# Splitting the planes of a burst around the next half round's first sum, in the two-tile stage of an FFT convolution

## The chip, the cores and the metric

The kernel runs on one core of one Trainium2 chip. The metric is the device time of one execution in microseconds (us); less is better. One core has a matrix engine (PE, with its weight loads shown as PEld), a vector engine (DVE), a scalar engine (ACT), a general engine (POOL) and a queue engine (SP) that issues the DMAs here. Every engine works through its own instructions strictly in the order in which the program gives them; engines wait for each other by semaphores.

## The reference

```
def reference(x, w):                       # x (1, 224, 224, 96), w (7, 7, 96, 96), bfloat16
    wp = jnp.pad(w, ((0, H - K), (0, W - K), (0, 0), (0, 0)))
    Xf = rfft2(x, axes=(1, 2)); Wf = rfft2(wp, axes=(0, 1))      # float32
    Yf = jnp.einsum('bhwi,hwio->bhwo', Xf, Wf)
    y = irfft2(Yf, s=(H, W), axes=(1, 2)).astype(jnp.bfloat16)
```

So it is a circular 7 x 7 convolution with 96 channels in and out on a picture of 224 x 224, with padding that wraps around.

## The kernel before

The rows of the picture are cut into 8 bands of 28 (`NJ`, `B`), each taken with 6 rows of its neighbour, so that a band has 34 values along h (`L`). Along h a band is transformed by a small real transform with 17 frequencies (`NS`); along w the convolution is done directly, pair of pixels by pair, with a scheme that saves products: it needs sums and differences of neighbouring columns, the planes. The width is cut into seven tiles of 32 columns (t = 0 to 6). Per tile there are four kinds of work:

- The forward transform: matmuls from the pixels `xn` with the matrix `Fm` into PSUM, evacuated to `xf` (`a_jobs`, `f_jobs`).
- The planes: `jit(t, g)` (line 476) makes, for a group of three frequencies, seven planes `J` from `xf` by three DVE instructions: four differences in one instruction (96x1824 for three frequencies, 96x1216 for two), one sum (96x456), and two sums of planes (96x912). There are three buffers `J`, used in turn.
- The products: `b_round(t, s, mid, end, ydve, planes)` (line 529), one call for each tile and frequency s. This text calls a call a half round. Its PE part is 19 matmuls into a PSUM bank `b0` (line 557), then the jobs of `mid()`, then 14 matmuls into a bank `b1`, then the jobs of `end()`. ACT reads `b0` into `tt_` (line 604), DVE makes the first sum `u` from `b0` and `tt_` (line 607), DVE makes `v` from `b1` and `tt_` (line 617), and POOL makes the result `yf` from `u` and `v` (`ysum`, line 620). The tiles `u`, `v` and `tt_` have two buffers each (`tv_pool`, line 779): the u of a half round is written into the place that the sum of the half round two earlier reads, and tt_ into the place that the v of two half rounds earlier reads. The two frequencies s = 0 and s = 16 (`REAL`) take a shorter path without u and POOL: DVE adds straight into `yf`.
- The inverse transform: `yf` goes through DRAM (`scr`), comes back as `tt` and is multiplied by `Gm`; the result is stored.

PSUM has eight banks; all banks come from one pool (line 106), and each new use of a bank waits until the readers of its last use are done. Which physical bank a use gets is settled when the program is built.

The order of the work is written out by hand. Tiles 0 and 1 are worked on together (the loop at line 816): in round r tile 0 does frequency r and tile 1 frequency r - 4 (`LAG`), so that most rounds have two half rounds, tile 0's ahead of tile 1's. In this two-tile stage the remaining weights are prepared as well: matmuls from `wq` (`prep_jobs`, line 349), evacuations into `WF`, and at the end of each group two or three DVE instructions `diff` (line 380, 96x960, WF<-WF). These, and the forward transform of tiles 1 and 2, are the jobs that `mid()` and `end()` hand out. From tile 2 on the tiles run one after the other (the loop at line 864).

The planes of a group are made in one half round, its burst: `bursts` (line 807) holds twelve of them, keyed by round and tile; eleven of them fall to tile 0 and tile 1 and the last one is `jit(2, 0)` in round 18. Two of the twelve come in REAL half rounds: round 4, tile 1 (s = 0), and round 16, tile 0 (s = 16). In a burst the planes follow v on DVE (line 629), and POOL's sum of that half round is made to wait for the last of them (line 634). They are wanted three half rounds later or more.

Who evacuates a bank, DVE or ACT, is decided when the program is built: `evac` (line 119) gives it to the engine with the smaller running estimate in `load`; every job and every plane instruction adds to that estimate at the moment at which it is recorded. At line 639 the finished `yf` of three frequencies is stored to `scr`, behind the jobs of `end()`.

Of the kernel before, what the change touches and what calls it, by code (L numbers as in the profile page):

```python
# [10 lines left out]
ALU = mybir.AluOpType  # L11
# [7 lines left out]
REAL = (0, NS - 1)  # L19
# [36 lines left out]
def kernel(  # L56
# [7 lines left out]
    _, H, W, C = x.shape  # L64
    assert tuple(w.shape) == (KT, KT, C, C) and C == 96 and H == NJ * B and W % (2 * TW) == 0
    NT = W // (2 * TW)
    TL = NT - 1
# [7 lines left out]
    SYNC = mybir.DependencyInfo(mybir.DependencyClass.Sync, mybir.DependencyReason.DATA)  # L75
# [19 lines left out]
    VE, SE, GE, TE, DE = (_Ordered(e) for e in (nc.vector, nc.scalar, nc.gpsimd, nc.tensor, nc.sync))  # L95
# [37 lines left out]
    def dma(out_ap, in_ap):  # L133
        return DE.dma_start(out=out_ap, in_=in_ap)

    WF = cpool.tile([128, NSLOT, NTAP, C], BF16, name="WF")
    PP = POS * NJ
# [123 lines left out]
    for r, n, v in ((0, 0, 1.0), (0, LC, -1.0), (1, 1, -1.0), (1, L - 1, 1.0)):  # L261
        o = mf[:, :, 2 * NS - 2 + r:2 * NS - 1 + r]
# [213 lines left out]
    def jit(t, g):  # L476
        s0, s1 = JGB[g]
        n = s1 - s0
        xf = xf_tiles[t][0:C]
        xv = xf.rearrange("c p r s w j -> c p r s (w j)")  # L480
        b = jcount[0] % 3 if t < 2 else (jcount[0] - 2 * len(JGB)) % 2
        jcount[0] += 1
        Jb = J_bufs[b][0:C].rearrange("c (k s q) -> c k s q", k=7, s=3)
        for s in range(s0, s1):
            jbuf[(t, s)] = Jb[:, :, s - s0]

        def sub(o, a, b, op, cost):
            def f():
                load["v"] += 170 + cost / 1.92
                return VE.tensor_tensor(out=o, in0=a, in1=b, op=op)  # L490
            return f
        x0, x1 = xv[:, 0, :, s0:s1], xv[:, 1, :, s0:s1]
        c0, c1 = max(s0, REAL[0] + 1), min(s1, REAL[1])
        i0, i1 = c0 - s0, c1 - s0
        pd, rd, sd, qd = x1.ap
        dpl = bass.AP(x1.tensor, x1.offset - NJ, [pd, [NJ, 2], rd, sd, qd])
        return [
            sub(Jb[:, 0:4, 0:n].rearrange("c (k r) s q -> c k r s q", r=2), dpl,
                x0.unsqueeze(1).to_broadcast([C, 2, 2, n, PP]), ALU.subtract, 4 * PP * n),
            sub(Jb[:, 4, i0:i1], xv[:, 0, 0, c0:c1], xv[:, 0, 1, c0:c1], ALU.add, PP * (c1 - c0)),  # L500
            sub(Jb[:, 5:7, i0:i1], Jb[:, 0:4:2, i0:i1], Jb[:, 1:4:2, i0:i1], ALU.add, 2 * PP * (c1 - c0)),
        ]
# [16 lines left out]
        return ops  # L519

    yf_cur = {}

    def pairs(ap):
        return ap.rearrange("p (r g o) -> p g r o", r=2, o=2)

    def yp(ap):
        return ap.rearrange("p g (r o) -> p g r o", o=2)

    def b_round(t, s, mid, end, ydve=False, planes=()):
        xf = xf_tiles[t][0:C]  # L530
        Jb = jbuf[(t, s)]
# [9 lines left out]
        else:  # L541
# [3 lines left out]
            yf, y0, y1 = yf_cur[t]  # L545
# [14 lines left out]
        if s in REAL:  # L560
            for part in range(2):
                conv(b0, part * C, 0, part)
            if t == TL:
                SE.copy(out=tt_.rearrange("p (r m o) -> p r m o", r=2, m=2),
                        in_=b0[:, 0:2 * C].rearrange("p (r o) -> p r o", o=C).unsqueeze(2).to_broadcast([128, 2, 2, C]))
            else:
                SE.copy(out=tt_[:, 0:2 * C], in_=b0[:, 0:2 * C])
            mid()
            for mi, m in enumerate((2, 1)):
                for part in range(2):  # L570
                    conv(b1, (part * 2 + mi if t == TL else mi * 2 + part) * C, m, part)
            if t == TL:
                VE.tensor_tensor(out=yp(ym), in0=pairs(tt_[:]), in1=pairs(b1[:, 0:4 * C]), op=ALU.add)
            else:
                VE.tensor_tensor(out=ym,
                                 in0=tt_[:, 0:2 * C].rearrange("p (r o) -> p r o", o=C).unsqueeze(1).to_broadcast([128, 2, 2, C]),
                                 in1=b1[:, 0:4 * C].rearrange("p (m r o) -> p m r o", m=2, r=2), op=ALU.add)
            load["a"] += 110 + 0.9 * 192
            load["v"] += 540
            for f in planes:  # L580
                f()
            end()
        else:
            v = tv_pool.tile([128, 2, 2, C], F32, name="v")
            if merge:
                conv(b0, 2 * C, 0, 0, both=True)
                conv(b0, 2 * C, 2, 0, add=True)
                conv(b0, 3 * C, 1, 0, add=True)
                conv(b0, 0, 0, 1)
                conv(b0, C, 0, 2)  # L590
                SE.mul(out=tt_[:], in_=b0[:, 0:4 * C], mul=-0.5)
                u, pr = tt_[:, 2 * C:4 * C].rearrange("p (m o) -> p m o", m=2), tt_[:, 0:2 * C]
            else:
                for part in range(3):
                    conv(b0, part * C, 0, part)
                conv(b0, 3 * C, 2, 0)
                conv(b0, 4 * C, 1, 0)
                u = tv_pool.tile([128, 2, C], F32, name="u")
                if t == TL:
                    SE.mul(out=tt_[:, 0:C], in_=b0[:, 0:C], mul=-0.5)  # L600
                    SE.copy(out=tt_[:, C:3 * C], in_=b0[:, C:3 * C])
                    load["a"] += 240
                else:
                    SE.mul(out=tt_[:, 0:3 * C], in_=b0[:, 0:3 * C], mul=-0.5)
                pr = tt_[:, C:3 * C]
            if not merge:
                VE.scalar_tensor_tensor(out=u[:], in0=b0[:, 3 * C:5 * C].rearrange("p (m o) -> p m o", m=2), scalar=-0.5,
                                        in1=tt_[:, 0:C].unsqueeze(1).to_broadcast([128, 2, C]), op0=ALU.mult, op1=ALU.add)
            mid()
            for mi, m in enumerate((2, 1)):  # L610
                for pi, part in enumerate((1, 2)):
                    conv(b1, (pi * 2 + mi if t == TL else mi * 2 + pi) * C, m, part)
            if t == TL:
                VE.tensor_tensor(out=v[:], in0=pr.rearrange("p (r o) -> p r o", r=2).unsqueeze(2).to_broadcast([128, 2, 2, C]),
                                 in1=b1[:, 0:4 * C].rearrange("p (r m o) -> p r m o", r=2, m=2), op=ALU.add)
            else:
                VE.scalar_tensor_tensor(out=v.rearrange("p m r o -> p m (r o)"),
                                        in0=pr.unsqueeze(1).to_broadcast([128, 2, 2 * C]), scalar=-2.0,
                                        in1=b1[:, 0:4 * C].rearrange("p (m q) -> p m q", m=2), op0=ALU.mult, op1=ALU.add)
            def ysum(eng):  # L620
                if t == TL:
                    return eng.tensor_tensor(out=yp(ym), in0=pairs(v.rearrange("p r m o -> p (r m o)")),
                                             in1=u.rearrange("p m (g o) -> p (m g) o", o=2).unsqueeze(2).to_broadcast([128, C, 2, 2]), op=ALU.add)
                return eng.tensor_tensor(out=ym, in0=v[:],
                                         in1=u.unsqueeze(2).to_broadcast([128, 2, 2, C]), op=ALU.add)
            if ydve:
                ysum(VE)
            last = None
            for f in planes:
                last = f()  # L630
            if not ydve:
                y = ysum(GE)
                if last is not None:
                    tc.add_manual_dep(y.ins, last.ins.name, SYNC, reason="sum after planes")
            load["a"] += 490 if merge else 410
            load["v"] += (560 if ydve else 250 if t < 2 else 0) + (560 if merge else 900)
            end()
        if t != TL and s == y1 - 1:
            dma(scr_tiles[t].rearrange("w j s e -> (w j) s e")[:, y0:y1], yf[:, 0:y1 - y0].rearrange("p s r m o -> p s (r m o)"))

    scr_tiles = {}
# [29 lines left out]
    def turn_a(i):  # L671
        src = xn_all[:, 0:NA].bitcast(F32).rearrange("p (g k s) -> p g k s", k=2, s=SR)
        turn(src, xs[:, 0:NA], i * C // 8, (i + 1) * C // 8)
# [96 lines left out]
    last = [f() for f in fj[0][1]]  # L770
# [3 lines left out]
    for f in jit(0, 0):  # L774
        f()
# [40 lines left out]
    for r in range(NS + LAG):  # L816
# [31 lines left out]
        for t in range(2):  # L848
            s = r - LAG * t
            if not 0 <= s < NS:  # L850
                continue
            now = bursts.pop((r, t), ())
            now = jit(*now) if now else ()
# [10 lines left out]
    for t in range(2, NT):  # L864
# [19 lines left out]
        for s in range(NS):  # L884
            now = ()
            if s in plan:
                g = plan[s]
                now = jit(t, g + 1) if g + 1 < len(JGB) else jit(t + 1, 0)
# [5 lines left out]
            if t == TL and s in LROUND:  # L894
                now = late_planes(LROUND[s])
            if t == TL and s >= SA:
                if s < NS - 1:
                    now = [lambda i=s - SA: turn_a(i)]
# [30 lines left out]
    for i, (j, h) in enumerate(order):  # L929
# [3 lines left out]
        k = i + 8 - LF  # L933
# [38 lines left out]
```

## Time and profile before

| What | Before |
|---|---|
| Median of 3 runs | 264.38 us (264.13 to 265.65) |
| The profiled execution's own time | 264.4 us |
| Its span in the profile | 262.7 us |
| PE, busy share of the span | 96% |
| DVE | 81% |
| ACT | 76% |
| POOL | 40% |

The span is the time from the first to the last instruction that the profiler saw; 1.7 us of the execution's own time lie around it. A busy share is an average over the whole span. The page also has a chain of waits: from the last instruction back, at every step to what released it. Nearly all instructions carry line 88 in the profile, the line of the wrapper that records them, so they are told apart by what they write and read, as in `J<-xf`. All times of places in this text are us from the start of the span.

### The profile page before, as it was taken

The numbers are of one execution on the slowest core, as the hardware profiler recorded it, in microseconds if no ns is written. First come the engines' busy times: TensorE is split into PE (matmuls) and PEld (weight loads), VectorE is DVE, ScalarE is ACT, GpSimd is POOL, SyncE is SP. The second block draws the span as 40 slices with busy tenths as digits, with TensorE's granted clock in tenths as the row PEclk, the third lists the DMA queues.
The fourth block names the chain that finished last, engine by engine and source line by source line (L and its number), as shares of the span: only waits on it lengthen the run. The fifth ranks groups of instructions, "written<-read, shape, count | busy, mean of one in ns | idle before, by whom it ended". The sixth has DMA issues, their size and how long they took to land.

```text
span 262.7 us, 12200 instructions
## 1 busy us (share of the span) xinstructions
PE 251.7 (96%) x5156; PEld 233.9 (89%) x5156; DVE 214.0 (81%) x456; ACT 198.4 (76%) x500; POOL 106.3 (40%) x170
## 2 busy tenths in 40 slices
PE   8899898999999999999999999999999999999981
PEld 3679898999999999999999998999999999999861
DVE  5657899897979969977988788777978889889982
ACT  5558897659785666998988879989798886666662
POOL 7782042336355652234133322643143222555621
PEclk9999999999999999999999999999999999999998
DMA  6848010641111299997978549698959853495145
GB/s 167 250 124 218 11 49 2 170 146 50 47 47 47 95 267 191 259 246 201 299 222 216 162 128 302 195 265 204 297 190 209 228 160 134 131 175 167 52 116 175
DMA packets 41416, 43.44 MB, mean 165 GB/s; under 512 B 30836, under 2 KB 33104, under 8 KB 41362
## 3 DMA queue, kind: packets, MB, share of 16 engines
q1 hardware_dynamic: 41044, 41.98, 57.8%
q8 instruction: 40, 0.66, 1.1%
q0 software_dynamic: 192, 0.52, 0.7%
q10 hardware_dynamic: 126, 0.17, 0.2%
q14 instruction: 14, 0.11, 0.1%
HBM read 22.09 MB, written 19.66 MB: 159 GB/s over the span
## 4 chain that ended last, share of the span: by engine, by line
PE 76%; POOL 7%; DVE 7%; issue 5%; ACT 4%; DVEq 0%; POOLq 0%; ACTq 0%
PE pb L88 76%; POOL ct L88 6%; DVE WF L88 2%; ACT WF L88 2%; DVE J L88 1%; DVE u L88 1%; ACT xf L88 1%; DVE xf L88 1%; DVE v L88 1%; POOL yf L88 1%; DVE yf L88 0%; ACT tt L88 0%; ACT tt__1860 L88 0%; ACT ct L88 0%; ACT tt__2947 L88 0%
## 5 line engine op out<-in xcount | busy, mean ns | idle before, releaser
L88 PE MATMUL pb<-WF,J 96*128 96x96 bf16 x2782 | 160.4, 206 | 0.8 <-DVE WF L88 0.7
L88 PEld LDWEIGHTS <-J 96*128 96x128 bf16 x2782 | 136.1, 98 | 9.0 <-DVE u L88 1.5
L88 POOL TENSOR_TENSOR yf<-v,u 128x384 bf16<-128x384 f32 x70 | 69.7, 1009 | 128.0 <-issue 68.5
L88 ACT CAST xf<-pb 96x408 bf16<-96x408 f32 (+3 forms) x143 | 67.1, 488 | 9.0 <-PE pb L88 7.2
L88 PE MATMUL pb<-WF,xf 96*128 96x96 bf16 x991 | 61.7, 206 | 1.1 <-ACT xf L88 0.5
L88 DVE TENSOR_TENSOR J<-xf 96x1824 bf16<-96x1824 bf16 (+1 forms) x82 | 56.9, 732 | 0.1
L88 PEld LDWEIGHTS <-xf 96*128 96x128 bf16 x991 | 49.0, 98 | 2.0 <-issue 1.0
L88 PE MATMUL pb<-Fm,xn 118*128 118x136 bf16 (+3 forms) x640 | 45.5, 199 | 0.9 <-DVE u L88 0.8
L88 ACT CAST WF<-pb 96x480 bf16<-96x480 f32 (+1 forms) x59 | 29.1, 573 | 4.5 <-PE pb L88 4.5
L88 PE MATMUL pb<-tt,Gm 102*84 102x384 bf16 (+1 forms) x132 | 32.1, 326 | 0.0
L88 PEld LDWEIGHTS <-xn 118*128 118x128 bf16 x640 | 30.5, 97 | 1.2 <-issue 1.1
L88 ACT CAST yo<-pb 84x384 bf16<-84x384 f32 (+1 forms) x66 | 28.2, 484 | 2.9 <-PE pb L88 2.9
L88 ACT CAST J<-pb 84x384 bf16<-84x384 f32 (+1 forms) x65 | 28.0, 484 | 3.0 <-PE pb L88 3.0
L88 DVE TENSOR_TENSOR J<-J 96x912 bf16<-96x912 bf16 (+2 forms) x41 | 22.5, 548 | 0.0
L88 PE MATMUL pb<-wq 98*128 98x120 bf16 (+1 forms) x288 | 21.3, 226 | 0.2 <-issue 0.2
L88 PEld LDWEIGHTS <-wq 98*128 98x128 bf16 x288 | 19.3, 148 | 0.6 <-issue 0.6
L88 POOL TENSOR_TENSOR xn<-v,u 128x384 bf16<-128x384 f32 x12 | 10.9, 923 | 9.5 <-DVE J L88 6.5
L88 PEld LDWEIGHTS <-Gm 102*84 102x84 bf16 (+1 forms) x132 | 11.1, 117 | 1.0 <-DMA tt<-scr 0.2
L88 DVE TENSOR_TENSOR yf<-v,u 128x384 bf16<-128x384 f32 x20 | 11.3, 567 | 0.7
L88 PE MATMUL pb<-wu 128*128 128x512 bf16 x39 | 10.6, 432 | 1.1 <-DVE ct L88 1.1
L88 ACT COPY xf<-xf 96x816 bf16<-96x816 bf16 (+3 forms) x20 | 11.2, 622 | 0.0
L88 DVE CAST WF<-pb 96x480 bf16<-96x480 f32 (+1 forms) x13 | 7.5, 611 | 4.3 <-PE pb L88 4.1
(404 smaller groups left out, 253.9 us busy)
## 6 DMA issues: line engine op xcount, KB each, us to landing
scr<-yf SPq DMA_DIRECT2D x30, 288.0 KB
xn<-in_x_dram SPq DMA_DIRECT2D x12, 672.0 KB
tt<-scr SPq DMA_DIRECT2D x24, 336.0 KB
out_dram<-yo SPq DMA_DIRECT2D x12, 252.0 KB
out_dram<-J SPq DMA_DIRECT2D x12, 252.0 KB
tt<-scr SPq DMA_DIRECT2D x6, 288.0 KB
WF<-in_x_dram SPq DMA_DIRECT2D x2, 672.0 KB
scr<-yf SPq DMA_DIRECT2D x6, 192.0 KB
```

Of the source, the lines that this page charges most:

```text
L88: r = fn(*a, **k)
```

## The change

In tiles 0 and 1 the first plane instruction (four planes) is cut into two instructions of two planes. In a half round with u and with planes, in the two-tile stage, only the first instruction of the planes' list is recorded behind v; `end()` follows, and everything else of the burst (the other plane instructions, POOL's sum, and the store to `scr`, if the half round closes a group) is put into a list `rest`. The next half round records it right behind its u and ahead of its `mid()`. In the two REAL bursts all plane instructions stay together. For `jit(2, 0)` the first instruction is not cut; the two others move. In the later tiles the planes stay where they were, but the store to `scr` is recorded ahead of `end()` now.

```
@@ jit
+        cut = ((0, 2),) if t > 1 else ((0, 1), (1, 2))
         return [
-            sub(Jb[:, 0:4, 0:n].rearrange("c (k r) s q -> c k r s q", r=2), dpl,
-                x0.unsqueeze(1).to_broadcast([C, 2, 2, n, PP]), ALU.subtract, 4 * PP * n),
+            sub(Jb[:, 2 * a:2 * b, 0:n].rearrange("c (k r) s q -> c k r s q", r=2), dpl[:, a:b],
+                x0.unsqueeze(1).to_broadcast([C, b - a, 2, n, PP]), ALU.subtract, 2 * (b - a) * PP * n) for a, b in cut] + [
...
+    rest = []
+
+    def go_on():
+        while rest:
+            rest.pop(0)()
...
@@ b_round, both paths
+            go_on()
             mid()
...
@@ b_round, path with u
-            last = None
-            for f in planes:
-                last = f()
-            if not ydve:
-                y = ysum(GE)
-                if last is not None:
-                    tc.add_manual_dep(y.ins, last.ins.name, SYNC, reason="sum after planes")
+            now = min(len(planes), 1) if t < 2 else len(planes)
+
+            def finish():
+                last = None
+                for f in planes[now:] if now < len(planes) else ():
+                    last = f()
+                if not ydve:
+                    y = ysum(GE)
+                    last = last or done[0]
+                    if last is not None:
+                        tc.add_manual_dep(y.ins, last.ins.name, SYNC, reason="sum after planes")
+                if t != TL and s == y1 - 1:
+                    dma(scr_tiles[t].rearrange("w j s e -> (w j) s e")[:, y0:y1], yf[:, 0:y1 - y0].rearrange("p s r m o -> p s (r m o)"))
+            done = [None]
+            for f in planes[0:now]:
+                done[0] = f()
+            if now < len(planes):
+                rest.append(finish)
+            else:
+                finish()
...
             end()
-        if t != TL and s == y1 - 1:
+        if t != TL and s == y1 - 1 and s in REAL:
             dma(scr_tiles[t].rearrange("w j s e -> (w j) s e")[:, y0:y1], yf[:, 0:y1 - y0].rearrange("p s r m o -> p s (r m o)"))
```

On DVE a burst so goes from "v, planes, u of the next half round" to "v, half of the first, u of the next half round, the other half, the other two".

More of the change, by code (lines that the diff above doesn't have):

```diff
@@ L608, in b_round @@
                                         in1=tt_[:, 0:C].unsqueeze(1).to_broadcast([128, 2, C]), op0=ALU.mult, op1=ALU.add)
+            go_on()
             mid()
```

## The prediction

> **What bounds the kernel now.** I read the page first: the shares of the engines and the chain of waits.
>
> ```profile
> span 262.7 us, 12200 instructions
> ...
> PE 251.7 (96%) x5156; PEld 233.9 (89%) x5156; DVE 214.0 (81%) x456; ACT 198.4 (76%) x500; POOL 106.3 (40%) x170
> ...
> PE 76%; POOL 7%; DVE 7%; issue 5%; ACT 4%; DVEq 0%; POOLq 0%; ACTq 0%
> ```
>
> PE sets the time: whatever makes it stand still is added to the end, and a faster DVE is worth only the stalls that it takes away. The change works from 20 to 97 us, so I cut that into windows (us, then busy us and instruction counts for PE, PEld, DVE, ACT, POOL, then clock and DMA).
>
> ```profile
> 20.00:35.00 15.00, 13.97 (x328) 13.77 (x329) 12.69 (x24) 13.55 (x34) 3.45 (x5) 1.00 0.40 101
> 35.00:50.00 15.00, 14.01 (x348) 13.78 (x344) 14.18 (x28) 10.92 (x29) 4.02 (x4) 1.00 0.22 68
> 50.00:65.00 15.00, 14.91 (x338) 14.79 (x337) 13.29 (x26) 11.99 (x29) 6.92 (x8) 1.00 0.36 112
> 65.00:80.00 15.00, 14.95 (x343) 14.86 (x340) 12.58 (x24) 11.66 (x28) 6.87 (x7) 1.00 0.12 46
> 80.00:97.00 17.00, 17.00 (x457) 17.00 (x455) 14.89 (x34) 9.83 (x27) 10.04 (x11) 1.00 0.43 130
> ```
>
> PE has 2.2 us of idle time in these 77 us, nearly all before 50; from 50 on it is full, with DVE at 84 to 89%. There is little to win and a nearly full DVE to disturb. PE's timeline shows the largest stall that a late u causes:
>
> ```profile
> 44.96 0.95 PE L88 MATMUL pb<-Fm,xn 118*128 118x32 bf16 x32 [0.80 <-DVE u L88]
> ```
>
> A stall is a little longer start to start: 0.96 here, 0.24 at 60.1 and 0.21 at 71.1, 1.4 us in all. Then one burst, on DVE and on POOL:
>
> ```profile
> 56.11 0.54 DVE L88 SCALAR_TENSOR_TENSOR v<-tt__1547,pb 128x384 f32<-128x384 f32 x1
> 56.58 1.70 DVE L88 TENSOR_TENSOR J<-xf 96x1824 bf16<-96x1824 bf16 x2
> 58.20 0.62 DVE L88 TENSOR_TENSOR J<-J 96x912 bf16<-96x912 bf16 x1
> 58.74 0.34 DVE L88 SCALAR_TENSOR_TENSOR u<-pb,tt__1592 128x192 f32<-128x192 f32 x1
> 59.01 0.54 DVE L88 SCALAR_TENSOR_TENSOR v<-tt__1592,pb 128x384 f32<-128x384 f32 x1
> 60.00 0.36 DVE L88 SCALAR_TENSOR_TENSOR u<-pb,tt__1653 128x192 f32<-128x192 f32 x1 [0.45 <-POOL yf L88]
> ```
>
> ```profile
> 56.00 1.00 POOL L88 TENSOR_TENSOR yf<-v,u 128x384 bf16<-128x384 f32 x1 [2.19 <-DVE v L88]
> 58.95 2.95 POOL L88 TENSOR_TENSOR yf<-v,u 128x384 bf16<-128x384 f32 x3 [1.95 <-issue]
> ```
>
> The u right behind the planes (58.74) is late, but the next one (60.00) is later still: it waits for POOL's sum, which waits for the planes, and PE's stall at 60.1 hangs on this u.
>
> **The change, part by part.** Steps on DVE, start to start, from its timeline: 1824-element difference 1.02, 456-element sum 0.31, 912-element plane sum 0.54, u 0.27, v 0.46, an evacuation into WF 0.56. POOL's sum takes 1.00 and starts 0.12 behind the planes.
>
> *The cut.* The half (912 elements, from xf) is in no row. Bounds: half of 1.02 (0.51) and the 912-element sum that waits for its forerunner (0.62). I take the line through 1824 and 456 elements: 0.07 + 0.52 per thousand, 0.54. So each of eleven cuts adds 0.07 (0 to 0.2). It lies beside PE's work unless DVE is the one waited for.
>
> *The u that comes forward* gains up to 1.3 us. This frees its bank sooner, worth the 0.21 at 71.1. It isn't worth the 0.96: that burst is the REAL one of round 4, which keeps its planes together.
>
> *The rest that goes behind it.* The last planes and POOL's sum come later by u and the cut, 0.34. Where tt_ isn't there when the half is done, DVE also stands idle with planes behind it. At 61.9 the half ends its step at 62.45 and tt_ comes at 62.79: 0.43 with the signal. At 74.95 it is 0.35, at 49.8 0.13, and at 93.8, where the whole first instruction stays ahead, 1.07. Queued behind the waiting u are the planes, v, and the mid jobs; POOL's sum waits for the planes, the u after next for POOL's sum.
>
> *The DMAs.* Stores to scr now stand in SP's queue ahead of a round's output stores and loads of tt and xn, and may hold these by about one POOL sum (1.0). I cost this at nothing: the loads wait for PE to free their buffers anyway, and the one matmul that waited for SP (0.2 at 230.7) has an unchanged order in front of it. Without that cover it is up to 1.0 once per tile. The order on POOL is unchanged.
>
> *The evacuations.* The extra planes entries in the estimate shift them. In the built order DVE has one WF evacuation more between 31 and 45 and two fewer from 45 to 49; two more go to ACT near 200 us. Banks also come out in another order from 33 us on; that I can only bound: nothing, or a few stalls of the kind seen (0.2 to 0.5 each).
>
> Now the new order written out with these steps, place by place; what counts is where PE meets a late bank or plane.
>
> 1. 33 to 46: DVE is full here. One more evacuation 0.56, waiting for ACT, which has one more ahead of tt_, 0.39, three cuts 0.21, POOL in the way 0.10: the u at 44.57 ends at 46.17 instead of 44.91. In the new order of banks this holds the matmul that started at 45.76: PE +0.46.
> 2. 49 to 61: one evacuation less brings DVE to the u 0.45 ahead of tt_, so the planes end at 52.70, two sums of POOL run to 54.8, and the weights' WF<-WF behind them shift by 0.5. That lag meets the burst above: its 456-element plane ends at 59.60, wanted at 59.07; planes 60.14, POOL 61.27, u 61.64, so the matmul of 60.41 starts at 61.69. PE +0.82.
> 3. 61 to 74: the same with idle 0.43 and WF<-WF again: a late v costs 0.17, the second burst's u behind POOL (74.83) 0.5 to 0.7, and the 0.21 is gained. PE +0.65.
> 4. 74 to 85: a 152-element plane is 0.57 late.
> 5. 85 to 90: a 456-element plane is 0.53 late; its margin was 0.27.
> 6. 93 to 106: the late planes of tile 2 meet margins of 0.29. PE +0.4.
>
> Places 1 to 3 give 1.93. Places 4 to 6 give 1.5 and rest on a lag carried through several bursts; DVE has idle times there that can swallow part, so I take two thirds, 1.0. Sum 2.9: span 265.6, with the 1.7 around it 267.3. The profiled execution's own 264.4 is the median's 264.38, so nothing is to be corrected.
>
> How POOL and DVE get in each other's way is in the rows: WF<-WF takes 0.64 alone and 0.96 at 53.36, where it ends 0.51 behind POOL's sum. The Trainium skill, page "SBUF — State Buffer", section "Who interferes with whom", says that a VectorE instruction with two SBUF inputs contends with a GpSimd one that reads SBUF, and that the one issued first keeps the shared ports for its whole instruction. By that rule every POOL sum pushed into WF<-WF blocks them, as the trace agrees (1.65 instead of 1.10 for J<-xf at 42.14); this speaks against the change. Were there no blocking, WF<-WF would start with u in places 2 to 4, some 0.6 earlier each, and place 1 would lose 0.1: a sum near 1.0.
>
> **Rivals.**
>
> *The slack holds (not slower).* Most banks are freed 1 to 2 us ahead of their next use between 62 and 97, and planes wait there up to 2.0 us for their matmul. If no lag is carried from burst to burst, only single shifts of 0.34 remain: 0.34 at 60.1, 0.46 at 46, less 0.21, about 0.1 for the margin of 0.27. That is +0.7, 265.1. It decides if DVE regains the lag, 0.5 us, before the next burst. For it: idle of 0.4 to 0.8 in front of several u. Against: in place 2 and 3 WF<-WF uses that idle up.
>
> *The u sets the stalls (faster).* If the banks held by u were all that PE waits for, the 1.4 us would go: 263.0. It decides if PE's next wait at 46 and 60 comes over 0.5 sooner. Against: two of the three stalls are the REAL burst's and POOL's.
>
> *The changed banks and evacuations cost further on.* Four to ten stalls of 0.2 to 0.5 in the one-tile stage, where DVE is over 80% busy as well: +2 to +3 on top, 269.5 to 270.5. For it: at 105.5 and 157.8 PE already waits for u there. Against: the order of the work is the same.
>
> **How the numbers follow.** Forecast 0.55 (266.0 to 269), slack 0.27 (264.4 to 266), faster 0.07, further on 0.11. A measurement of this kernel tells about 1% (2.6 us) from no change, so the bound lies at 267.0, inside the forecast's range: of its 0.55 I put 0.40 above. Slower 0.40 + 0.11 = 0.51, same 0.15 + 0.27 + 0.06 = 0.48, faster 0.01, since all three stalls together are half a per cent. Range 264.4 to 269.6: it leaves out the faster case and most of the worst one.
>
> **What would show it.** In the changed profile: u right behind the half, and a wait for ACT's tt_ ahead of it where I gave one; planes ending 0.3 to 1 later against PE; DVE u waiting for POOL in more than four places between 20 and 97; PE waiting for J at about 59 and 90; PE's stall at 44 moved, not gone. It would be wrong if PE's idle time from 50 to 97 stays below 1 us.

## The result, and the profile after

| | Before | After |
|---|---|---|
| Median | 264.25 us (264.1 to 268.09, 6 runs) | 268.08 us (267.7 to 269.18, 6 runs) |
| Ratio, 95% interval | | 1.0145 (1.0125 to 1.0165) |
| The profiled execution's own time | 264.4 us | 269.18 us |
| Its span | 262.7 us | 267.5 us |

The change costs 3.8 us. One of the six runs before took 268.09 us; the other five lie between 264.1 and 265.65. The page of the changed kernel, span and chain of waits:

```profile
span 267.5 us, 12212 instructions
...
PE 59%; DVE 14%; issue 10%; POOL 9%; ACT 5%; DVEq 0%; POOLq 0%
```

PE's share of the chain falls from 76 to 59%, DVE's doubles: the chain now leaves PE more often. The same windows as before (us, then busy us and counts for PE, PEld, DVE, ACT, POOL, clock and DMA):

```profile
50.00:65.00 15.00, 14.51 (x315) 14.13 (x312) 12.79 (x27) 10.83 (x26) 5.93 (x6) 1.00 0.41 132
65.00:80.00 15.00, 14.63 (x332) 14.44 (x329) 12.57 (x27) 11.91 (x27) 6.19 (x7) 1.00 0.12 43
80.00:97.00 17.00, 16.32 (x428) 15.92 (x426) 14.72 (x35) 8.86 (x25) 10.24 (x11) 1.00 0.26 87
```

PE had 0.14 us idle in these three, now it has 1.54. The matmuls fall from 1138 to 1075, and 63 of them at the 0.042 us of the commonest are 2.6 us: part of the waiting is booked as busy. PE's timeline shows both kinds:

```profile
43.08 0.93 PE L88 MATMUL pb<-WF,J 96*128 96x96 bf16 x18 [0.63 <-DVE v L88]
...
58.80 1.23 PE L88 MATMUL pb<-WF,J 96*128 96x96 bf16 x18
...
61.79 0.39 PE L88 MATMUL pb<-Fm,xn 118*128 118x64 bf16 x8 [0.32 <-DVE u L88]
...
74.96 0.63 PE L88 MATMUL pb<-wq 98*128 98x120 bf16 x8 [0.36 <-DVE u L88]
...
82.23 0.33 PE L88 MATMUL pb<-WF,xf 96*128 96x96 bf16 x4 [0.29 <-DVE WF L88]
...
90.37 0.34 PE L88 MATMUL pb<-WF,J 96*128 96x96 bf16 x4 [0.37 <-DVE J L88]
...
109.39 0.33 PE L88 MATMUL pb<-WF,J 96*128 96x96 bf16 x4 [0.27 <-DVE u L88]
```

The row at 58.80 has no bracket, but its 18 matmuls take 1.23 where the 18 at 43.08 take 0.93: the 0.3 is a wait for a late plane in the middle of the group. So starts of the same matmul are compared instead, which the unchanged order on PE allows:

| Place | The same matmul, before and after | Lag of PE | Step | Step as predicted |
|---|---|---|---|---|
| 1 | 45.76, 46.31 | 0.55 | 0.55 | 0.46 |
| 2 | 60.41, 61.79 | 1.38 | 0.83 | 0.82 |
| 3 | 72.95, 74.96 | 2.01 | 0.63 | 0.65 |
| 4 | 82.90, 85.48 | 2.58 | 0.57 | 0.57 |
| 5 | 87.24, 90.37 | 3.13 | 0.55 | 0.53 |
| 6 | 105.82, 109.39 | 3.57 | 0.44 | 0.4 |

The predicted steps of places 4 to 6 are those before the prediction took two thirds of them. With 0.22 more at 153 us this makes 3.8, the difference of the medians. The profiled execution has 1.02 more, a pause of PE at 125.3 with no releaser in the trace; the profiles of two variants with the same work there (e4, e9) don't have it, and I leave it out.

DVE at the burst that the prediction showed (there 56.58 to 60.00):

```profile
57.59 0.92 DVE L88 TENSOR_TENSOR J<-xf 96x912 bf16<-96x912 bf16 x1
58.44 0.34 DVE L88 SCALAR_TENSOR_TENSOR u<-pb,tt__1594 128x192 f32<-128x192 f32 x1
58.71 0.92 DVE L88 TENSOR_TENSOR J<-xf 96x912 bf16<-96x912 bf16 x2
59.55 0.62 DVE L88 TENSOR_TENSOR J<-J 96x912 bf16<-96x912 bf16 x1
...
61.38 0.36 DVE L88 SCALAR_TENSOR_TENSOR u<-pb,tt__1659 128x192 f32<-128x192 f32 x1 [0.74 <-POOL yf L88]
```

The burst itself starts 1.01 later (57.59, was 56.58). Even so the u behind the half starts 0.30 earlier (58.44, was 58.74), a gain of 1.31 within the burst. The last plane instruction starts 1.35 later (59.55, was 58.20), so the burst adds 0.34 to the 1.01, and the next u starts 1.38 later (61.38, was 60.00), waiting 0.74 for POOL's sum instead of 0.45. It is this second u that holds PE's bank at 61.79. DVE's waits from 20 to 101 us (total, times, longest):

```profile
DVE u L88 <- POOL yf L88: 4.4, 7, 0.7
```

For the same work before, 20 to 97 us, it was 1.5 us in 4 waits.

### The profile page after: what moved, and what is told of

Same layout as the page of the kernel before. It is cut to its first block, busy times and chain, and to the rows that moved or that the text cites. A ratio compares the mean times of both kernels' runs of the same rounds, so it can differ in the third digit from the quotient of the medians.

```text
span 267.5 us, 12212 instructions
## 1 busy us (share of the span) xinstructions
PE 254.3 (95%) x5156; PEld 234.8 (88%) x5156; DVE 215.5 (81%) x465; ACT 199.4 (75%) x503; POOL 105.6 (39%) x170
## 4 chain that ended last, share of the span: by engine, by line
PE 59%; DVE 14%; issue 10%; POOL 9%; ACT 5%; DVEq 0%; POOLq 0%
PE pb L88 59%; POOL ct L88 6%; DVE J L88 4%; DVE WF L88 4%; POOL yf L88 3%; ACT WF L88 2%; DVE u L88 2%; DVE v L88 2%; ACT xf L88 1%; DVE xf L88 1%; DVE yf L88 1%; ACT tt L88 0%; ACT tt__673 L88 0%; ACT tt__1421 L88 0%; ACT tt__4411 L88 0%
## 5 line engine op out<-in xcount | busy, mean ns | idle before, releaser
L88 ACT CAST xf<-pb 96x408 bf16<-96x408 f32 (+3 forms) x146 | 68.3, 486 | 8.5 <-PE pb L88 5.1
L88 DVE TENSOR_TENSOR J<-xf 96x1824 bf16<-96x1824 bf16 (+5 forms) x94 | 58.9, 662 | 0.1
```

Source lines behind the costliest of these rows:

```text
L88: r = fn(*a, **k)
```

## The experiments

The theory on trial: the planes behind the next u, and POOL's sum behind them, come late by u and by the wait for tt_, and PE has no slack to take it up. Rivals: the cut itself, the shifted evacuations, the stores. All kernels are timed beside the kernel before; PE's lag is the difference of the same matmul's start between 33 and 106 us, 3.50 in the changed kernel.

| Kernel | Median, us | Ratio to before, 95% interval | Lag of PE, 33 to 106 us |
|---|---|---|---|
| e1, cut alone | 264.51 | 1.0002 (0.9993 to 1.0011) | 0.11 |
| e2, moved, not cut | 266.55 | 1.0081 (1.0064 to 1.0098) | 1.81 |
| e3, stores alone | 265.36 | 1.0027 (1.0015 to 1.0039) | 0.22 |
| e4, evacuations as before | 268.59 | 1.0172 (1.0140 to 1.0204) | 3.78 |
| e5, sum free of planes | 266.39 | 1.0075 (1.0050 to 1.0100) | 1.51 (see e5) |
| e6, three u | 266.46 | 1.0063 (1.0040 to 1.0087) | 2.04 |
| e7, late bursts alone | 266.88 | 1.0083 (1.0058 to 1.0108) | 2.44 |
| e8, early bursts alone | 266.56 | 1.0069 (1.0044 to 1.0094) | 1.96 |
| e9, stores back | 268.25 | 1.0140 (1.0126 to 1.0154) | 3.50 |
| b9, one REAL burst moved | 263.52 | 0.9967 (0.9955 to 0.9980) | -0.65 |
| b10, the same and three u | 263.16 | 0.9949 (0.9935 to 0.9962) | -1.02 |

**e1, the cut alone.** The kernel before, with `cut` in `jit`; the planes' estimates are added in one sum, as large as before, at the burst (e2, e4, e7 and e8 do the same).

```
+ cut = ((0, 2),) if t > 1 else ((0, 1), (1, 2))
- sub(Jb[:, 0:4, 0:n]..., dpl, x0..., ALU.subtract, 4 * PP * n),
+ sub(Jb[:, 2 * a:2 * b, 0:n]..., dpl[:, a:b], x0..., ALU.subtract, ...) for a, b in cut] + [
```

> The kernel before with the cut alone: the first plane instruction is two of 912 elements, nothing is moved, and the evacuations are shared out as before. Theory (planes and POOL's sum reach PE late, because they stand behind the next u and behind its wait for tt_): the cut is worth only 0.07 us on DVE per burst, eleven times, and most of it lies beside PE: 264.3 to 264.8. Rival (the cut itself is the cost: the half is dearer than the line through 1824 and 456 elements gives, and DVE is full): 265.5 to 267.

264.51, a ratio of 1.0002. Taken together the cut alone costs nothing that can be measured. In the trace PE loses 0.44 us in steps of 0.15 or less and wins 0.33 in round 4, where the stall of 0.96 falls to 0.61.

**e2, moved but not cut.** The changed kernel with the whole first instruction ahead of u.

```
- cut = ((0, 2),) if t > 1 else ((0, 1), (1, 2))
+ cut = ((0, 2),)
```

> The changed kernel without the cut, the evacuations shared out as before: the whole first plane instruction stays ahead of the next u, the other two and POOL's sum stand behind it. Theory: tt_ is there when DVE comes to u, so DVE idles less ahead of u than with the half, the planes come later by one u (0.27) and not by 0.34 and more, u gains 0.85 and not 1.3; about half of the change's loss: 265.5 to 266.8. Rival (the cut is the cost): 264.3 to 265.

266.55: the move, with the new place of the stores, costs 2.2, and the cut, free when alone, another 1.5 to 2.0 on top of it. DVE's timeline shows why. The first burst of place 3 (61.91 before), first in e2, then in the changed kernel:

```profile
62.46 1.10 DVE L88 TENSOR_TENSOR J<-xf 96x1824 bf16<-96x1824 bf16 x1
63.48 0.35 DVE L88 SCALAR_TENSOR_TENSOR u<-pb,tt__1786 128x192 f32<-128x192 f32 x1
...
64.05 0.62 DVE L88 TENSOR_TENSOR J<-J 96x912 bf16<-96x912 bf16 x1
```

```profile
63.29 0.62 DVE L88 TENSOR_TENSOR J<-xf 96x912 bf16<-96x912 bf16 x1
64.19 0.36 DVE L88 SCALAR_TENSOR_TENSOR u<-pb,tt__1792 128x192 f32<-128x192 f32 x1 [0.28 <-ACT tt__1792 L88]
...
65.31 0.62 DVE L88 TENSOR_TENSOR J<-J 96x912 bf16<-96x912 bf16 x1
```

The whole instruction covers the time in which ACT makes tt_; u follows with no wait. The half is too short for that, and DVE waits 0.28 with planes queued behind the u: from the first plane instruction's start to the last one's start 2.02 us instead of 1.59. Place by place the picture is the same. Against e2, e4 (the same cut and move, evacuations as in e2) has larger steps of PE by 0.60, 0.28, 0.52 and 0.51 in places 1 to 4 and by 0.06 and 0.00 in places 5 and 6. Its longest waits for tt_ behind a half are in places 1, 3 and 4 (0.71, 0.28, 0.28); in place 5 it has none, and in place 6 nothing is cut.

**e3, the stores alone.** The kernel before, with the store in front of `end()` in half rounds with u.

```
+            if t != TL and s == y1 - 1:
+                dma(scr_tiles[t]...[:, y0:y1], yf[:, 0:y1 - y0]...)
             load["a"] += 490 if merge else 410
...
-        if t != TL and s == y1 - 1:
+        if t != TL and s == y1 - 1 and s in REAL:
```

> The kernel before with the new place of the stores to scr alone: ahead of the jobs of end() in the half rounds with u, no plane moved and none cut. Theory: nothing, 264.0 to 264.6. Rival (a store that waits for POOL's sum holds the output stores and the loads behind it in SP's queue, up to one sum of 1.0 us per tile): 265 to 268.

The rival: 0.7 us by the ratio, 1.0 by the medians. SP's queue before, and below it in e3 (the DMAs' issues):

```profile
91.83 2.51 SPq L88 DMA_DIRECT2D xn<-in_x_dram  x3
```

```profile
91.98 0.32 SPq L88 DMA_DIRECT2D xn<-in_x_dram  x1
96.81 0.34 SPq L88 DMA_DIRECT2D scr<-yf  x1
97.24 1.33 SPq L88 DMA_DIRECT2D xn<-in_x_dram  x2
```

A store stands between the loads now (before it follows them, at 96.65) and waits 4.4 us for POOL's sum; the last two loads of pixels, and behind them the loads of tt, start late, and PE stands in front of a matmul with tt:

```profile
105.06 0.49 PE L88 MATMUL pb<-tt,Gm 102*84 102x384 bf16 x2 [0.27 <-DMA tt<-scr]
```

Start to start it is 0.43; another 0.22, for a u, appears at 149. The profiled execution took 264.78, little more than the kernel before, so its trace shows only a part of the 0.7 to 1.0.

**e4, the evacuations as before.** The changed kernel; `est[0]`, the planes' whole estimate without the cut's share, is added where the burst is recorded.

```
-                load["v"] += 170 + cost / 1.92
...
+        est[0] = 510 + PP * (4 * n + 3 * (c1 - c0)) / 1.92
...
+            planned(planes)
             load["a"] += 490 if merge else 410
```

> The changed kernel with DVE and ACT sharing the evacuations exactly as before: a burst's estimate is added at the burst and without the cut's share. Theory: the evacuation into WF that came to DVE between 31 and 45 us is worth up to the first step of the lag, 0.55 of 3.6, the rest stays: 267.2 to 268. Rival (the shifted evacuations start the lag, and the planes alone would fit into the slack): 264.5 to 266.

268.59, above the theory's 268: nothing is gained. The evacuation that came to DVE at place 1 did not cost its 0.56, and the reason is in the same stretch of DVE's timeline, first e4, then the changed kernel:

```profile
38.65 0.36 DVE L88 SCALAR_TENSOR_TENSOR u<-pb,tt__1040 128x192 f32<-128x192 f32 x1 [0.71 <-ACT tt__1040 L88]
```

```profile
37.99 0.65 DVE L88 CAST WF<-pb 96x480 bf16<-96x480 f32 x1
```

In the changed kernel the evacuation lies between the half and the u; without it DVE waits there 0.71 for ACT. The u starts at about the same time either way (38.56 and 38.65), and PE's step at place 1 is no smaller in e4 (0.63 against 0.47).

**e5, the sum free of the planes.** The changed kernel; POOL's sum is recorded behind v.

```
             now = min(len(planes), 1) if t < 2 else len(planes)
+            if now < len(planes) and not ydve:
+                ysum(GE)
...
-                if not ydve:
+                if now == len(planes) and not ydve:
```

> The changed kernel with POOL's sum of a burst recorded right behind its v and free of the planes; the planes stay split as in the change. Theory (the lag reaches PE through two things, the planes and POOL's sum behind them): the waits of u for POOL (stalls of 0.21 at 46, 0.49 at 61, 0.17 and 0.52 at 72 and 74, 0.43 at 109, 1.8 together) fall away, the late planes (0.29 at 59, 0.18 at 85, 0.53 at 90, 0.17 at 103, 1.2 together) stay, and may grow by the time in which the sum and the half get in each other's way: 265.5 to 266.7. Rival (all of it goes through DVE's own queue, POOL's sum is late only because the planes are): 267.5 to 268.5.

266.39, as the theory has it: by the medians 1.7 of the 3.8 us went with the sum's lateness. The lags can't be compared over the whole stretch. The profiled execution took 268.75; PE loses 2.9 us in it before 33 us, of which 1.4 in front of one matmul that waits for a load (until 17.0), and at place 1 it makes up 0.61 where the changed kernel loses 0.47. From 46 to 106 us PE falls back 2.12 in e5 and 3.03 in the changed kernel. The small wait for u at place 1 (0.21) is still there. The waits for u at 61 and 72 to 74 and for WF at 55 and 82 are gone or no longer than 0.2, the waits for planes at 61, 86 and 91 are longer (0.80, 0.72 and 0.64, in the changed kernel 0.29, 0.18 and 0.53). The last part shows in DVE's and then POOL's timeline of e5:

```profile
59.07 0.92 DVE L88 TENSOR_TENSOR J<-xf 96x912 bf16<-96x912 bf16 x1
...
60.19 1.48 DVE L88 TENSOR_TENSOR J<-xf 96x912 bf16<-96x912 bf16 x2
```

```profile
58.50 2.37 POOL L88 TENSOR_TENSOR yf<-v,u 128x384 bf16<-128x384 f32 x2 [2.19 <-DVE v L88]
```

The half takes 0.92 beside POOL's sum and 0.62 without one (63.29 above); the second half and the 456-element plane behind it take 1.48 where the changed kernel shows 0.92 or 0.93. The Trainium skill, page "SBUF — State Buffer", section "Who interferes with whom", has these two as excluding one another, the first issued going first; the trace agrees, since POOL's first sum ends at 59.5 and the half 0.5 behind it.

**e6, three places for u.** The changed kernel.

```
+    tu_pool = ctx.enter_context(tc.tile_pool(name="tu", bufs=3))
...
-                u = tv_pool.tile([128, 2, C], F32, name="u")
+                u = tu_pool.tile([128, 2, C], F32, name="u")
```

> The changed kernel with three places for u instead of two, so that a u does not wait for the sum of the half round two earlier. Theory: the same 1.8 of stalls by u shrink, but the weights' WF<-WF still meet POOL's late sum (stalls 0.2 at 55 and 0.46 at 82 stay) and the planes are still late: 266 to 267. Rival (the wait for POOL is only the last link, DVE is late anyway): 267.5 to 268.5.

266.46, the theory again. No u waits for POOL, and v waits a little in its stead (DVE's waits, 20 to 112 us; in the changed kernel 5.2 us for u there):

```profile
DVE v L88 <- POOL yf L88: 1.6, 4, 0.5
```

Gone are the stalls at 61 (0.49) and 74 (0.52), and of the WF ones at 55 and 82 no more than 0.12 is left, since DVE comes to WF<-WF earlier; the planes' stalls at 59.6 (0.31) and 88.8 (0.53) stay, and the one at 84.0 grows from 0.18 to 0.41. Contrary to the expectation, the stalls for WF<-WF shrank too, though nothing but u's third place was changed.

**e7 and e8, half of the bursts each.** The changed kernel with evacuations as before; `mv[0]` is `r >= 8` in e7 and `r < 8` in e8.

```
- now = min(len(planes), 1) if t < 2 else len(planes)
+ now = min(len(planes), 1) if t < 2 and mv[0] else len(planes)
```

> Evacuations as before, and planes split and moved only in the bursts of round 8 and later (from 61 us on); the four early bursts as before. Theory one (each burst adds its own lag, because PE has no slack to give back and each burst finds too little margin of its own): the steps from 61 us on add up to 2.2 to 2.4 as in the full change: 266.3 to 267. Theory two (DVE carries its lag from burst to burst, so that places 4 to 6 are only late because 1 to 3 were): 264.9 to 265.9.

> The complement: evacuations as before, and planes split and moved only in the four bursts before round 8 (to 61 us). Theory one: the lag of PE reaches 1.4 to 1.9 at 61 us and stays there: 265.7 to 266.3, and this run's loss and that of the late bursts alone add up to the whole change's. Theory two: DVE's lag at 61 us runs on into the later bursts although their own planes are not moved: 266.6 to 268. Third possibility (PE gives the lag back where it waited before): 264.3 to 265.3.

Theory one, by the traces of both. In e7 the steps at 73, 83, 87 and 106 are 0.71, 0.60, 0.55 and 0.55, as large as in the full change, though no earlier burst was moved. PE's waits there in e7:

```profile
73.78 0.66 PE L88 MATMUL pb<-wq 98*128 98x120 bf16 x8 [0.38 <-DVE u L88]
...
81.07 0.33 PE L88 MATMUL pb<-WF,xf 96*128 96x96 bf16 x4 [0.27 <-DVE WF L88]
...
89.21 0.34 PE L88 MATMUL pb<-WF,J 96*128 96x96 bf16 x4 [0.37 <-DVE J L88]
...
108.34 0.33 PE L88 MATMUL pb<-WF,J 96*128 96x96 bf16 x4 [0.27 <-DVE u L88]
```

The median of e7, 266.88, lies in theory one's range; that of e8, 266.56, lies just above it and just below theory two's. In e8 PE's lag is 1.51 at 60 and still 1.51 at 87: it is neither given back nor does it breed more. 2.44 and 1.45 (e8 up to 87) make 3.89, e4 has 3.78. What e8 loses further on begins with a wait for a load of tt, the price of the stores as in e3:

```profile
106.73 0.49 PE L88 MATMUL pb<-tt,Gm 102*84 102x384 bf16 x2 [0.58 <-DMA tt<-scr]
```

**e9, the stores back.** The changed kernel; only a store whose sum is held over stays in front.

```
-                if t != TL and s == y1 - 1:
+                if t != TL and s == y1 - 1 and now < len(planes):
...
-        if t != TL and s == y1 - 1 and s in REAL:
+        if t != TL and s == y1 - 1 and (s in REAL or not now < len(planes)):
```

> The changed kernel with the stores to scr back behind the jobs of end(), in every half round whose planes are not held over. The new place alone was worth 0.7 to 1.0 us in the kernel before, where PE waited 0.43 us for a load of tt at 104.6. Theory (in the changed kernel PE comes to that load 3.5 us late and no matmul waits for SP there, so the store's price is hidden; only the 0.22 at 153, seen in all runs with the new place and not in before, goes): 267.5 to 268.2. Rival (the store's price is part of the measured 3.8): 266.8 to 267.4.

268.25 against 268.08, no difference; the stall of 0.22 at 153 is gone, as expected. In the changed kernel the lag of 3.5 covers the late loads; e7, whose lag is 2.3 there, doesn't wait for that load either, while e8 with 1.5 does. The costs of the parts do not add up: the stores are worth 0.7 to 1.0 alone and nothing behind the late planes.

**b9 and b10, a version that beats both.** The largest stall before (0.96 at 44) is the burst that the change leaves as it was. b9 is the kernel before with that burst alone moved, whole, behind the next u; b10 adds the three places for u.

```
-            for f in planes:
-                f()
+            if (t, s) == (1, 0):
+                rest.extend(planes)
+            else:
+                for f in planes:
+                    f()
...
                                        in1=tt_[:, 0:C]..., op0=ALU.mult, op1=ALU.add)
+            while rest:
+                rest.pop(0)()
             mid()
```

> The kernel before with one burst moved, the one that the change leaves in place: in round 4's REAL half round of tile 1 all three plane instructions stand behind the next half round's u instead of ahead of it. No cut, no other burst, stores as before; POOL's sum is not part of a REAL half round, so nothing of POOL's is moved. Theory (the 0.96 stall at 44 is the u standing behind 2.2 us of planes, and these have three half rounds to their first use): the u comes 2.2 earlier and most of the stall goes, the planes come 0.27 later: 263.3 to 263.9. Rival (PE's stall only moves to the next bank, as in the changed kernel, where it became 0.79 for v): 264.1 to 264.8.

> The same as the one before, and three places for u. Theory (the stall of 0.24 at 60 is a u that waits for POOL's sum, which is late behind the planes; with three places it need not wait): 0.2 less than the kernel with the moved burst alone: 263.1 to 263.7. Rival (without the wait the u is held by DVE's queue all the same): no difference between the two.

263.52 and 263.16. In b9 the u starts at 42.34 (44.57 before) and PE's matmuls follow one another there; first DVE's row, then PE's:

```profile
42.34 0.36 DVE L88 SCALAR_TENSOR_TENSOR u<-pb,tt__1156 128x192 f32<-128x192 f32 x1 [0.17 <-ACT tt__1156 L88]
```

```profile
43.94 0.96 PE L88 MATMUL pb<-Fm,xn 118*128 118x32 bf16 x32
```

Of the 0.97 won here 0.32 is given back at 45.06, where PE now comes ahead of an evacuation that stands behind the planes as before. The third place for u takes away the stall at 60 (0.21 in b9) and 0.16 of the 0.23 at 105: the intervals of b9 and b10 still overlap a little, the difference at the two stalls is plain in the traces.

## Why the prediction was right, and where it was wrong

Its forecast, slower by way of late planes and a late POOL sum, holds: 268.08 for 267.3, inside the range. Slack (265.1) and faster (263.0) did not come about; nor did the fourth case, whose stalls in the one-tile stage amount to one of 0.22, which e9 lays to the stores. (That case's time was also added up 0.2 too high: 267.3 and 2 to 3 make 269.3 to 270.3.) The signs that the prediction named came: u right behind the half, with a wait for tt_ at 64.19; u waiting for POOL in seven places; PE waiting for planes at 59.7 and 90.4; PE's stall at 44 moved, not gone; 1.54 us idle on PE from 50 to 97.

- *The u that comes forward is worth the 0.21 at 71.1 and not the 0.96.* Right. The 0.21 went, but a new wait for a u just ahead of it (72.03) takes 0.18 back. The stall of 0.96 moved: 0.79 stands at 42.3, for v, and 0.21 at 46.1, for a u.
- *The rest that goes behind it, 0.34 and the wait for tt_.* Right: 0.34 at the burst of 57.59, and waits, as the time by which u starts later than the instruction ahead of it lets it, of 0.36, 0.36, 0.36 and 1.16 (at 64.19, 77.84, 51.04 and 99.08) where 0.43, 0.35, 0.13 and 1.07 were forecast. The wait, which the cut brings, is a little under half of the loss: e2 has the move without most of it and loses 2.2 instead of 3.8. The half was priced at 0.54 a step, and e1 shows 0.54 (62.25 to 62.79); what a shorter first instruction does besides is to uncover ACT.
- *Places 1 to 3, 1.93.* Measured 2.01, of which 0.08 stood before 33 us. In place 1 a part of the cause was wrong: the 0.56 of an evacuation filled a wait for tt_ instead of coming on top of it, and without it (e4) PE's step is no smaller. That 0.46 met 0.47 there is partly luck.
- *Places 4 to 6, 1.5, of which two thirds were taken.* This is the step that failed. They measure 0.57, 0.55 and 0.44, 1.56 in all, and the discount of 0.5 is most of the 0.8 between forecast and result. It rested on "a lag carried through several bursts" that DVE's idle time could swallow. e7 shows that nothing has to be carried: late bursts alone make the same steps. The idle times are there, but ahead of u's that wait for tt_ or for POOL's late sum (0.70 at 80.74 and at 86.81 in the changed kernel), so that, as these rows read, they come with the lag and don't take it up.
- *Place 4's cause.* A plane of 152 elements was named; about 0.4 of the step is a WF<-WF behind POOL's sum (82.23 above), 0.18 a late plane. The mechanism of place 2, not seen for this place; that the step came out at the 0.57 forecast is luck. In place 6 about half of the 0.44 is a late plane, as forecast, and half a u that comes late (109.39 above).
- *The DMAs at nothing.* Right for this kernel by luck of the cover: alone they cost 0.7 to 1.0 (e3), once, not per tile, and the late PE hides it (e9). The cover was named wrongly: it is PE's own lag, not its hold on the loads' buffers.
- *The evacuations.* Worth nothing that can be measured (e4). What another order of the banks is worth by itself was not tried.
- *POOL and DVE in each other's way.* e5 and e6 remove different links and each takes somewhat less than half of the loss by the medians (1.7 and 1.6 of 3.8), so the way through POOL's sum and the third u is shown; that without any blocking the sum would be "near 1.0" was not tried.

Open: the pause at 125.3 in one execution, the part of the stores' 0.7 to 1.0 that e3's trace doesn't show, and what place 1 costs in an execution of e5 without the early loss.

## What to carry to other kernels

When an engine that sets the time is full, work moved behind another instruction costs what that instruction takes and also what it waits for: look at what its operand's maker is doing at that moment, because a shorter piece ahead may just uncover that wait. Price every place where the bound engine meets a late result as a step of its own, and add the steps whole; idle time on the late engine is no reserve if it lies ahead of an instruction that waits for someone else. Move one thing where the trace shows the stall (b9) rather than a class of things by a rule, and see which buffer count makes one engine's lateness another's.

## What the runs showed of the hardware

- The half, a DVE instruction with two inputs from SBUF, and POOL's sum did not run beside each other: the half takes 0.62 alone and 0.92 with 0.4 us of a sum still to run, and ends 0.5 behind it; v, with one input in PSUM, takes 0.54 in both cases (58.61 in e5's stretch, beside the sum). The prediction had this; the size of the other side, that a sum free of the planes meets them and makes them later, was not foreseen (PE waits 0.80 and 0.72 for them in e5, 0.29 and 0.18 in the changed kernel).
- A DMA issue that waited for its data held the issues behind it in SP's queue: 4.4 us in e3, of which PE felt 0.43.
